# Heads, weight products and small loads of a branchformer backward kernel put in a hand-written order

## The chip, the cores and the metric

The kernel runs on one core of one Trainium2 chip. The metric is the device time of one execution in microseconds (us). The engines are called PE (TensorE, matrix products), PEld (its weight loads), DVE (VectorE), ACT (ScalarE), POOL (GpSimd) and SP (SyncE, which here only issues DMAs). Each engine works through its own queue of instructions in order and waits at an instruction until what it needs is there.

## What is computed

One layer and its gradients for x of shape (2, 4000, 144) in bf16. Two branches share a layer norm of x: an attention branch and a local branch with a gate and a convolution over 5 neighbours in time. Their results are merged by another convolution of 5 taps and a product. The kernel returns the output and the gradients of x and of all seven weights.

```python
xa = layernorm(x)
q, k, v = split(xa @ w_qkv)
glob = softmax(q k^T / sqrt(D)) v @ w_att_out
u, g = split(gelu(xa @ w_mlp_in))
loc = (u * conv5(layernorm(g), dw_csgu)) @ w_mlp_out
m = concat(glob, loc)
out = x + (m + conv5(m, dw_merge)) @ w_merge
# outputs: out, and d/d(x, w_qkv, w_att_out, w_mlp_in, dw_csgu, w_mlp_out, dw_merge, w_merge) for a given grad_out
```

## The kernel before

Time steps are tiled in 32 blocks of 128 rows; 4 blocks make a group, so there are 8 groups (NGR). The two batch entries are worked one after the other. Each has three phases: `phase_head`, `phase_attn` and `phase_tail`.

*Weights.* `Weights.first` loads the weights, transposes them on PE (`turn`, L1139, one PSUM tile and one DVE copy L1140 for each piece) and forms folded products (`fused`, L1148): M1 from the query and key weights, WvoT, and GL, which holds for each of the 5 taps the merge weights times a branch weight times the tap's factor. For GL, the branch weights are first scaled by each tap's factor: `A` for branch 0 on DVE (L1221), `A` for branch 1 and the small `Bz` on POOL (L1223, L1224), one instruction for each tap. `Weights.second` makes what is first needed later: transposes of Wo, Wi and Wm, the diagonals `w_dg` and `c80` of the convolution (`c80` from `w80`, ten DMAs of 16 elements), a flag (whether the fast path is allowed), WIM, copies of weights to DRAM, and G (ten products and ten ACT copies, L1337 and L1149, after ten small copies on POOL, L1332).

*Head.* For each group: `stA` takes `gs`, a load of grad_out rows with all 5 neighbours (720 KB, three slots, issued on SP by `take_go`), transposes its middle row (L1425), copies the 16 narrow columns together on POOL (`g80`, L1428) and transposes those (L1431, into go80, L1434). In batch 0 it also forms the norm of x: `stats` (DVE, L1367 and L1368), `power` (POOL, L1375 and L1376), `apply` (L1383 to L1388, on ACT, DVE and POOL); in batch 1 these were done in the tail before. `stT` transposes the normed x (L1439, L1443). `stB` handles two blocks: the query product pq (L1459, L1460) and pb (5 products L1467 and one L1468), copied out by DVE and ACT. Eight of the sixteen stB are done in the head; the rest are placed in the first rows of attention.

*Attention.* A written-out loop over 32 rows of blocks: scores (L1861, L1865), the exponential (ACT), a product (DVE), transposes by DMA (`flip`, SP), then y (L1911) and X (L1933, L1934). A list of small steps (`local_steps`) fills in the local branch. The first instruction of attention on PE is the pS product of L1861.

*Tail.* Steps h = 0 to 20 over pairs of blocks: turns (L2039, L2041, L2074), correlations EF (L2063), output products (L2088, L2089) and dx products (L2106). Narrow rows go to DRAM and come back shifted by `Taps`: `put` stores them (L1520) and `fill` loads them (L1527), both issued on ACT. `Taps` also writes two zero columns at each end, by two DMAs when it is made (L1514, L1515). The tail of batch 0 also prepares the norm of batch 1. The tail of batch 1 forms the weight gradients (`Finish`).

*Order.* Inside `tc.manual_schedule()` the instructions are queued as the code has them. Attention's loop and the tail's loop stand inside it. The weights, the heads, `local_steps`' opening instructions and the making of the `Taps` stand outside: there a planner chooses the order of each queue by its own priorities.

Of the kernel before, what the change touches and what calls it, by code (L numbers as in the profile page):

```python
# [1120 lines left out]
class Weights:  # L1121
# [6 lines left out]
    def turn(self, src, R, c0, C, name, ps, pool=None):  # L1128
        nc = self.k.nc
        nk, nck = (R + 127) // 128, (C + 127) // 128  # L1130
        t = (pool or self.tmp).tile([128, nck, R], BF, name=name)
        if C % 128:
            nc.vector.memset(t[:, nck - 1, :], 0.0)
        for cc in range(nck):
            w = min(128, C - cc * 128)
            for kt in range(nk):
                rk = min(128, R - kt * 128)
                pt = ps.tile([128, 128], BF, tag="tp", name="pt")
                nc.tensor.transpose(pt[0:w, 0:rk], src[0:rk, kt, c0 + cc * 128:c0 + cc * 128 + w], self.W.ident[0:rk, 0:rk])  # L1139
                nc.vector.tensor_copy(t[0:w, cc, kt * 128:kt * 128 + rk], pt[0:w, 0:rk])  # L1140
        return t
# [12 lines left out]
    def first(self, ps, then):  # L1154

        k, W, tp_, nc, wp = self.k, self.W, self.tmp, self.k.nc, self.k.wp
        c = float(D) ** -0.5
        W.ident = wp.tile([128, 128], BF, name="w_ident")
        make_identity(nc, W.ident[:])
        ident = W.ident  # L1160

        def load_k(ap, R, C, name, engs):
            nk = (R + 127) // 128
            t = tp_.tile([128, nk, C], BF, name=name)
            if R % 128:
                nc.vector.memset(t[:, nk - 1, :], 0.0)
            for kt in range(nk):
                r0, r1 = kt * 128, min(R, kt * 128 + 128)
                engs[kt].dma_start(t[0:r1 - r0, kt, :], ap[r0:r1, :])
            return t  # L1170
        W.Wqkv = load_k(k.w_qkv, D, 3 * D, "w_qkv_s", (nc.sync, nc.scalar))
        W.Wo = load_k(k.w_att_out, D, D, "w_o_s", (nc.sync, nc.scalar))
        self.Wl = load_k(k.w_mlp_out, D, D, "w_l_s", (nc.sync, nc.scalar))
        Wmh = self.Wmh = tp_.tile([128, 2, 2, D], BF, name="w_mh")
        nc.vector.memset(Wmh[:, :, 1, :], 0.0)
        for h in range(2):
            nc.sync.dma_start(Wmh[:, h, 0, :], k.w_merge[h * D:h * D + 128, :])
            nc.scalar.dma_start(Wmh[0:DR, h, 1, :], k.w_merge[h * D + 128:h * D + D, :])
        cw = tp_.tile([5, 3 * D], BF, name="w_cw")
        nc.scalar.dma_start(cw[:, 0:2 * D], k.dw_merge)  # L1180
        nc.scalar.dma_start(cw[:, 2 * D:3 * D], k.dw_csgu)
        then()
        self.Wi = load_k(k.w_mlp_in, D, 2 * D, "w_i_s", (nc.sync, nc.scalar))

        WqT = self.WqT = self.turn(W.Wqkv, D, 0, D, "w_qT", ps)
        WkT = self.WkT = self.turn(W.Wqkv, D, D, D, "w_kT", ps)
        WqTz = tp_.tile([128, 2, 128], BF, name="w_qTz")
        nc.vector.memset(WqTz[:], 0.0)
        nc.vector.tensor_copy(WqTz[:, :, 112:128], WqT[:, :, 128:D])
        W.M1 = wp.tile([128, 2, D], BF, name="w_M1")  # L1190
        self.fused(ps, lambda kt: WqT[:, kt, :], self.two(WkT), c, 0, 128, W.M1[:, 0, :])
        self.fused(ps, lambda kt: WqTz[:, kt, :], self.two(WkT), c, 0, 128, W.M1[:, 1, :])
        WvT = self.WvT = self.turn(W.Wqkv, D, 2 * D, D, "w_vT", ps)
        WlT = self.turn(self.Wl, D, 0, D, "w_lT", ps)
        self.WvoT = tp_.tile([128, 2, D], BF, name="w_voT")
        self.vo(ps, self.WvoT, W.Wo, WvT)

# [4 lines left out]
        for n_, dst in enumerate((W.wm[:, 0], W.wm[:, 1], self.wcf[:])):  # L1202
            pt = ps.tile([128, 128], BF, tag="tp", name="pt")
            nc.tensor.transpose(pt[:, 0:5], cw[0:5, n_ * D:n_ * D + 128], ident[0:5, 0:5])
            nc.tensor.transpose(pt[0:DR, 6:11], cw[0:5, n_ * D + 128:n_ * D + D], ident[0:5, 0:5])
            nc.vector.tensor_copy(dst[:, 0, :], pt[:, 0:5])
            nc.vector.tensor_copy(dst[0:DR, 1, :], pt[0:DR, 6:11])
        nc.vector.tensor_scalar(W.wm[:, :, :, 2], W.wm[:, :, :, 2], 1.0, None, op0=ALU.add)

        UT = self.UT = [self.WvoT, WlT]  # L1210
        W.GL = wp.tile([128, 5, 2, D], BF, name="w_GL")
        W.GL80 = wp.tile([128, 2, D], BF, name="w_GL80")
        self.A = []
        for h in range(2):
            A = tp_.tile([128, 2, 5, D], BF, name="w_A%d" % h)
            self.A.append(A)
            Bz = tp_.tile([128, 2, 5, DR], BF, name="w_Bz%d" % h)
            for kt in range(2):
                for kk in range(5):
                    if h == 0:  # L1220
                        nc.vector.tensor_scalar(A[:, kt, 4 - kk, :], UT[h][:, kt, :], W.wm[:, h, kt, kk:kk + 1], None, op0=ALU.mult)  # L1221
                    else:
                        nc.gpsimd.tensor_scalar(A[:, kt, 4 - kk, :], UT[h][:, kt, :], W.wm[:, h, kt, kk:kk + 1], 1.0, op0=ALU.mult, op1=ALU.mult)  # L1223
                    nc.gpsimd.tensor_scalar(Bz[:, kt, 4 - kk, :], Wmh[:, h, kt, 128:D], W.wm[:, h, kt, kk:kk + 1], 1.0, op0=ALU.mult, op1=ALU.mult)  # L1224
            for (m0, m1) in ((0, 3), (3, 5)):
                pt = ps.tile([128, 512], F32, tag="w", name="fw")
                n = (m1 - m0) * D
                for kt in range(2):
                    nc.tensor.matmul(pt[:, 0:n], Wmh[:, h, kt, 0:128], A[:, kt, m0:m1, :].rearrange("p a b -> p (a b)"), start=(kt == 0), stop=(kt == 1))
                (nc.scalar.copy if m0 else nc.vector.tensor_copy)(W.GL[:, m0:m1, h, :], pt[:, 0:n].rearrange("p (a b) -> p a b", b=D))  # L1230
            pt = ps.tile([128, 512], F32, tag="w", name="fw")
            for kt in range(2):
                nc.tensor.matmul(pt[0:80, 0:D], Bz[:, kt, :, :].rearrange("p a b -> p (a b)"), UT[h][:, kt, :], start=(kt == 0), stop=(kt == 1))
            nc.scalar.copy(W.GL80[0:80, h, :], pt[0:80, 0:D])
        W.mhalf = wp.tile([128, 4], F32, name="w_mhalf")
        nc.vector.memset(W.mhalf[:], -0.5)

    def vo(self, ps, t, l, r):
        self.k.nc.vector.memset(t[:, 1, :], 0.0)
# [4 lines left out]
    def second(self, pst, ps):  # L1244
# [4 lines left out]
        w80 = tp_.tile([128, 2], BF, name="w_w80")  # L1249
        nc.vector.memset(w80[:], 0.0)  # L1250
        with nc.allow_non_contiguous_dma(reason="small conv weights, channel on partitions"):
            for m in range(5):
                nc.sync.dma_start(w80[m * DR:(m + 1) * DR, 0:1], k.dw_csgu[m:m + 1, 128:D].rearrange("o c -> c o"))
                nc.sync.dma_start(w80[m * DR:(m + 1) * DR, 1:2], k.dw_csgu[4 - m:5 - m, 128:D].rearrange("o c -> c o"))
        w80f = tp_.tile([128, 2], F32, name="w_w80f")
        nc.vector.tensor_copy(w80f[:], w80[:])

        W.Wi2 = wp.tile([128, 2, 2 * D], BF, name="w_i2")
        nc.vector.memset(W.Wi2[:, 1, :], 0.0)
        nc.sync.dma_start(W.Wi2[:, 0, :], k.w_mlp_in[0:128, :])  # L1260
        nc.sync.dma_start(W.Wi2[112:128, 1, :], k.w_mlp_in[128:D, :])
# [8 lines left out]
        W.c80 = wp.tile([128, 2, DR], BF, name="w_c80")  # L1270
        for v in range(2):
            nc.vector.tensor_scalar(W.c80[:, v, :], i80[:], w80f[:, v:v + 1], None, op0=ALU.mult)

        WoT = self.turn(W.Wo, D, 0, D, "w_oT", pst)
        WiT = self.turn(self.Wi, D, 0, 2 * D, "w_iT", pst)
        WmT = tp_.tile([128, 2, 2, D], BF, name="w_mT")
        nc.vector.memset(WmT[:, :, 1, :], 0.0)
        for h in range(2):
            for cc in range(2):
                w = 128 if cc == 0 else DR  # L1280
                for kt in range(2):
                    rk = 128 if kt == 0 else DR
                    pt = pst.tile([128, 128], BF, tag="tp", name="pt")
                    nc.tensor.transpose(pt[0:w, 0:rk], Wmh[0:rk, h, kt, cc * 128:cc * 128 + w], ident[0:rk, 0:rk])
                    nc.vector.tensor_copy(WmT[0:w, h, cc, kt * 128:kt * 128 + rk], pt[0:w, 0:rk])
        Wvo = tp_.tile([128, 2, D], BF, name="w_vo")
        self.vo(ps, Wvo, self.WvT, W.Wo)

        M1k = tp_.tile([128, 2, D], BF, name="w_M1k")
        nc.vector.tensor_copy(M1k[:], W.M1[:])  # L1290
        fro = tp_.tile([128, 2], F32, name="w_fro")
# [104 lines left out]
def phase_head(k, W, b, S, nrm, ld, wts):  # L1396

    nc, tc = k.nc, k.tc
    with ExitStack() as es:
# [15 lines left out]
        def stA(g):  # L1415
            if g not in S.gs:
                take_go(k, S, b, g, ld)
# [1152 lines left out]
```

## Time and profile before

| what | value |
|---|---|
| median of 4 runs | 1295.7 us (1294.82 to 1297.4) |
| profiled execution | 1296.55 us, span 1294.7 us |
| PE / PEld busy | 1215.6 us (94%) / 952.3 us (74%) |
| DVE / ACT / POOL busy | 960.5 / 843.6 / 558.3 us |
| instructions | 39900 |
| bytes moved by DMA | 205.51 MB, 159 GB/s on average |

Lines of code are given as L and a number. A wait line reads "who waited <- who released it: us in total, number of times, longest". In a line of stretches, the numbers after the length are busy us of PE, PEld, DVE, ACT and POOL with the number of instructions, then the granted clock of PE as a share of full speed, the busy share of the DMA engines and GB/s. Idle time of an engine costs something only if the engine, or someone waiting for it, sets the end.

### The profile page before, as it was taken

How to read it: one execution, taken by the hardware profiler on the slowest of the kernel's cores; microseconds unless marked ns; L12 is line 12 of the kernel's file. 1: busy time of each engine (PE TensorE's matmuls, PEld its weight loads, DVE VectorE, ACT ScalarE, POOL GpSimd, SP SyncE). 2: the span in 40 equal slices, each digit the busy share in tenths (PEclk: the TensorE clock that was granted, in tenths of full speed). 3: DMA queues.
4: the chain of work that ended last, by engine and by line, in shares of the span. 5: the costliest groups of instructions: out<-in, count | busy, mean ns of one | idle time of the engine just before them, and what ended most of it. 6: DMA issues, size and time to landing. Idle time of an engine off the chain costs nothing.

```text
span 1294.7 us, 39900 instructions
## 1 busy us (share of the span) xinstructions
PE 1215.6 (94%) x15116; PEld 952.3 (74%) x15116; DVE 960.5 (74%) x3293; ACT 843.6 (65%) x2498; POOL 558.3 (43%) x1033
## 2 busy tenths in 40 slices
PE   4899999999999999989989999999999999998996
PEld 2657777777777777789976777777777777778884
DVE  4656778888888788857735677888878878885674
ACT  2667677767767766546646777777777777654542
POOL 6312444545444453256611244444544445324650
PEclk9989999999999999999989999999999999999998
DMA  6368989898989989887765898999899899997861
GB/s 184 87 133 147 155 157 160 158 165 149 164 145 163 169 155 162 150 186 217 203 213 108 147 157 150 151 170 166 147 165 153 158 165 156 162 154 181 239 163 30
DMA packets 634223, 205.51 MB, mean 159 GB/s; under 512 B 577183, under 2 KB 631556, under 8 KB 633988
## 3 DMA queue, kind: packets, MB, share of 16 engines
q1 hardware_dynamic: 627472, 197.54, 79.9%
q10 hardware_dynamic: 6548, 5.33, 1.7%
q8 instruction: 120, 1.97, 0.6%
q14 instruction: 83, 0.68, 0.2%
HBM read 46.22 MB, written 21.79 MB: 53 GB/s over the span
## 4 chain that ended last, share of the span: by engine, by line
PE 70%; DVE 13%; DMA 6%; ACT 4%; issue 4%; POOL 2%; SPq 1%; ACTq 0%; DVEq 0%; POOLq 0%
PE y L1911 15%; PE pS L1865 9%; PE X L1933 8%; PE X L1934 8%; PE pD L1865 7%; DVE Sm L1875 5%; PE pS L1861 5%; PE pc L1573 2%; PE pb L1467 2%; DVE jg L1792 1%; PE po L2088 1%; DMA y<-r 1%; PE gr L2159 1%; PE EF L2063 1%; DMA ug<-ug_d 1%
## 5 line engine op out<-in xcount | busy, mean ns | idle before, releaser
L1875 DVE SCALAR_TENSOR_TENSOR Sm<-pD,Pm 128x500 bf16<-128x500 f32 x512 | 325.8, 673 | 80.9 <-PE pD L1865 47.7
L1873 ACT ACTIVATE Pm<-pS 128x500 bf16<-128x500 f32 x512 | 295.4, 586 | 41.2 <-PE pS L1865 38.3
L1933 PE MATMUL X<-Qs,Sm 128*128 128x144 bf16 x2048 | 285.6, 226 | 9.3 <-DVE acc L1949 8.9
L1946 POOL TENSOR_TENSOR acc<-xs,acc 128x432 f32<-128x432 f32 x150 | 168.6, 1124 | 280.6 <-ACT xs L1945 280.2
L1934 PE MATMUL X<-Bt,Pm 128*128 128x144 bf16 x2048 | 285.4, 226 | 0.7 <-DVE Bt L1898 0.7
L1934 PEld LDWEIGHTS <-Pm 128*128 128x128 bf16 x2048 | 200.2, 98 | 11.9 <-issue 11.3
L1933 PEld LDWEIGHTS <-Sm 128*128 128x128 bf16 x2048 | 200.1, 98 | 1.5 <-issue 0.9
L1911 PEld LDWEIGHTS <-PT 128*128 128x128 bf16 x2048 | 136.5, 98 | 31.1 <-issue 2.4
L1911 PEld LDWEIGHTS <-ST 128*128 128x128 bf16 x2048 | 136.4, 98 | 27.6
L1945 ACT COPY xs<-X 128x432 f32<-128x432 f32 x150 | 77.9, 519 | 111.7 <-PE X L1934 103.6
L1949 DVE TENSOR_TENSOR acc<-X,acc 128x432 f32<-128x432 f32 x180 | 104.0, 578 | 54.1 <-PE X L1934 53.4
L1873 ACT ACTIVATION_READ_ACCUMULATOR Pm<-pS 128x1 f32 x512 | 104.9, 205 | 0.0
L1861 PE MATMUL pD<-rb,QBr 16*128 16x500 bf16 x448 | 96.0, 378 | 3.3 <-DVE Sm L1875 2.8
L1865 PEld LDWEIGHTS <-BTm 128*128 128x128 bf16 x512 | 49.8, 98 | 59.9 <-issue 1.6
L1861 PE MATMUL pS<-rb,QBr 16*128 16x500 bf16 x448 | 92.0, 381 | 0.1
L1792 DVE SCALAR_TENSOR_TENSOR jg<-gnC,dgC 128x256 bf16<-128x256 bf16 x160 | 89.0, 556 | 1.0
L1921 POOL TENSOR_TENSOR B_t<-zd,yd 128x144 bf16<-128x144 f32 x64 | 33.8, 528 | 113.2 <-ACT zd L1920 112.9
L1865 PEld LDWEIGHTS <-QTm 128*128 128x128 bf16 x512 | 29.0, 97 | 72.8 <-issue 72.8
L1865 PE MATMUL pS<-rb,QTm 128*128 128x500 bf16 x256 | 76.9, 382 | 0.0
L1865 PE MATMUL pS<-ra,QTm 128*128 128x500 bf16 x256 | 76.5, 380 | 0.0
L1911 PE MATMUL y<-rb,PT 128*128 128x144 bf16 x1024 | 74.3, 226 | 1.4 <-ACT zd L1920 1.1
L1911 PE MATMUL y<-ra,PT 128*128 128x144 bf16 x1024 | 74.3, 226 | 1.1 <-ACT zd L1920 1.1
(626 smaller groups left out, 2898.6 us busy)
## 6 DMA issues: line engine op xcount, KB each, us to landing
gs<-in_grad_out_dram SPq DMA_DIRECT2D x24, 720.0 KB
dh_d<-dh SPq DMA_DIRECT2D x32, 144.0 KB
dhr<-dh_d SPq DMA_DIRECT2D x16, 288.0 KB
gs<-in_grad_out_dram SPq DMA_DIRECT2D x8, 540.0 KB
xg<-in_x_dram SPq DMA_DIRECT2D x21, 144.0 KB
dug_d<-dug SPq DMA_DIRECT2D x16, 144.0 KB
dug<-dug_d SPq DMA_DIRECT2D x32, 72.0 KB
ug_d<-ug SPq DMA_DIRECT2D x32, 72.0 KB
```

The costliest lines, as they stand in the source:

```text
L1792: nc.vector.scalar_tensor_tensor(jg[:], a_[:, m:m + 256], 1.0, d_[:, 2:258], op0=ALU.mult, op1=ALU.mult, accum_out=dws[:, p, m:m + 1])
L1861: nc.tensor.matmul(o_[h][:, 0:SC], jt[i // 4][2][rr, i % 4, :], S.XR[c2][rr, 0:SC], start=True, stop=False)
L1865: nc.tensor.matmul(o_[h][:, 0:SC], jt[i // 4][w][:, i % 4, :], S.xaT[:, c0:c0 + SC], start=False, stop=True)
L1873: nc.scalar.activation(P[:, pb, c1:c1 + SC], o_[h][:, 0:SC], ACT.Exp, accum_out=ld8[:, 0, n_:n_ + 1])
L1875: nc.vector.scalar_tensor_tensor(Sm[:, pb, c1:c1 + SC], o_[h][:, 0:SC], 1.0, P[:, pb, c1:c1 + SC], op0=ALU.mult, op1=ALU.mult, accum_out=l ...
L1911: nc.tensor.matmul(y[:, w, :], src[:, jj, :], S.xaa[:, j, :], start=(j == 0), stop=(j == NBK - 1))
L1921: nc.gpsimd.tensor_tensor(S.Zn[:, i, :], zd[:], yd[:], op=ALU.add)
L1933: nc.tensor.matmul(X[:, jj, :], Sm[:, i % NP, j * 128:(j + 1) * 128], Qs[:, i % 4, :], start=(kk == 0 and jj == 0), stop=False, skip_group ...
L1934: nc.tensor.matmul(X[:, jj, :], P[:, i % NP, j * 128:(j + 1) * 128], Bt[:, i % 4, :], start=False, stop=(kk == 1), skip_group_check=True)
L1945: nc.scalar.copy(xs[:, 0:nj, :], X[:, 0:nj, :])
L1946: nc.gpsimd.tensor_tensor(a_, xs[:, 0:nj, :], a_, op=ALU.add)
L1949: nc.vector.tensor_tensor(a_, X[:, 0:nj, :], a_, op=ALU.add)
```

## The change

1. The weights and both heads are put inside `tc.manual_schedule()`. `first` and `second` become `loads`, `heads`, `taps`, `taps1`, `keys`, `rows` and `rest`; `rest` is a generator, of which one piece is queued in each step of the head's loop.
2. `turn` collects a transposed weight in one PSUM tile and copies it out in one or two instructions. The tap products for all five taps become one tensor-tensor instruction for each half (`taps` on DVE, `taps1` on POOL, `Bz` goes from POOL to DVE). G is copied out by four wide copies.
3. x of batch 0 comes in three loads (group 0, groups 1 to 3, groups 4 to 7) in place of eight, and w_merge in two in place of four. The loads are issued in the order weights for q, k, v, x of group 0, the other weights, then gs and x by turns; Wi is loaded once, later.
4. `c80` is formed by two small products with a pattern matrix; the ten DMAs of `w80` are gone.
5. The norm is split in `stats`, `power`, `shift` and `apply`, in different steps. `g80` is formed ahead by `narrow_go`. In batch 0 DVE's share of `apply` goes to POOL, and every second copy of R goes from DVE to ACT. The head's PSUM pools have 4 and 3 tiles instead of 3 and 4.
6. In the tail the `Taps` are made after the first loads, `fill` of a group moves from the odd step after it to the beginning of the next even step, the norm of batch 1 lags by one step more, `take_go` for batch 1 moves to the end of its step, and two `narrow_go` for batch 1 are put in its last steps.
7. `local_steps` is called inside the manual order.

```diff
 class Weights: turn
-                pt = ps.tile([128, 128], BF, tag="tp", name="pt")
-                nc.tensor.transpose(pt[0:w, 0:rk], src[...], self.W.ident[0:rk, 0:rk])
-                nc.vector.tensor_copy(t[0:w, cc, kt * 128:kt * 128 + rk], pt[0:w, 0:rk])
+                nc.tensor.transpose(pt[0:w, cc, kt * 128:kt * 128 + rk], src[...], self.W.ident[0:rk, 0:rk])
+        n1 = C // 128
+        nc.vector.tensor_copy(t[:, 0:n1, :], pt[:, 0:n1, :])
+        if C % 128:
+            nc.vector.tensor_copy(t[0:C % 128, n1, :], pt[0:C % 128, n1, :])
...
+    def taps(self):
+        for kt in range(2):
+            nc.vector.tensor_tensor(self.A[0][:, kt], self.UT[0][:, kt, :].unsqueeze(1).to_broadcast([128, 5, D]),
+                                    self.wr[:, 0, kt, :].unsqueeze(2).to_broadcast([128, 5, D]), op=ALU.mult)
+        for h in range(2):
+            for kt in range(2):
+                nc.vector.tensor_tensor(self.Bz[h][:, kt], ..., op=ALU.mult)
+    def taps1(self, kt):
+        self.k.nc.gpsimd.tensor_tensor(self.A[1][:, kt], self.UT[1]..., self.wr[:, 1, kt, :]..., op=ALU.mult)
...
+            nc.tensor.matmul(pt[0:80, v * DR:(v + 1) * DR], e5[0:5].rearrange("p a b -> p (a b)"), self.cw[0:5, 2 * D + 128:3 * D], start=True, stop=True)
+            nc.vector.tensor_tensor(W.c80[0:80, v, :], pt[0:80, v * DR:(v + 1) * DR], i80[0:80, :], op=ALU.mult)
...
 phase_head
+        with tc.manual_schedule():
...
+            if wts:
+                wts.heads(ps_t, ps_2, lambda: nrm.stats(0))
+                nrm.power(0)
+                wts.taps1(0)
+                wts.keys(ps_t, ps_2)
+                nrm.shift(0)
+                nrm.apply(0)
+                narrow(0)
+                wts.taps()
+                wts.taps1(1)
+                nrm.stats(1)
+                nrm.power(1)
+                stA(0)
+                take_go(k, S, b, 3, ld)
+                stT(0)
+                wts.rows(ps_2, 0)
+                nrm.shift(1)
+                nrm.apply(1)
+                narrow(1)
+                nrm.stats(2)
+                nrm.power(2)
+                wts.rows(ps_2, 1)
+                rest = wts.rest(ps_t, ps_2)
...
+            for n in range(-1, NGR):
+                if 1 <= n + 2 < NGR:
+                    stT(n + 2)
+                if n >= 0:
+                    stB(n, *tiles())
+                if 1 <= n + 2 < NGR:
+                    stA(n + 2)
+                if wts and n + 3 < NGR:
+                    nrm.shift(n + 3)
+                    nrm.apply(n + 3)
+                if n + 3 < NGR:
+                    narrow(n + 3)
+                if wts and n + 4 < NGR:
+                    nrm.stats(n + 4)
+                    nrm.power(n + 4)
+                if n + 5 < NGR and n + 5 not in S.gs:
+                    take_go(k, S, b, n + 5, ld)
...
+                if n == 5:
+                    spread()
+                if n == 3:
+                    jit()
+                if rest:
+                    next(rest, None)
 phase_tail
-        taps = [Taps(k, "y80_%d" % b), Taps(k, "u80_%d" % b)]
...
             loads(1)
+            taps += [Taps(k, "y80_%d" % b), Taps(k, "u80_%d" % b)]
...
                     turn_dx2(*turn_dx(h))
+                if hf == 0 and 0 <= g - 2 < NGR:
+                    fill(g - 2)
...
-                if hf == 1 and 0 <= g - 1 < NGR:
-                    fill(g - 1)
...
-                    for lag, f_ in ((4, nrm.apply), (3, nrm.power), (2, nrm.stats), (1, nrm.load)):
+                    for lag, f_ in ((5, nrm.apply), (4, nrm.shift), (3, nrm.power), (2, nrm.stats), (1, nrm.load)):
...
-                    if NPR <= h < NPR + 3:
-                        take_go(k, nxt, 1, h - NPR, nrm.ld)
+                    if NPR + 3 <= h:
+                        narrow_go(k, nxt, h - NPR - 3, nrm.ld)
...
+                if nrm and NPR <= h < NPR + 3:
+                    take_go(k, nxt, 1, h - NPR, nrm.ld)
 bounded (loads of batch 0)
+                        def put(n):
+                            if n == 0:
+                                nc.vector.memset(S.Sm[:, 1, 15 * D:16 * D], 0.0)
+                                wide(0, 1)
+                                return
+                            take_go(k, S, 0, 0, nrm.ld)
+                            wide(1, 4)
+                            take_go(k, S, 0, 1, nrm.ld)
+                            wide(4, NGR)
+                            take_go(k, S, 0, 2, nrm.ld)
```

## The prediction

> **What bounds the kernel now.** I read the page first: TensorE (PE) is busy 1215.6 of 1294.7 us, so only what leaves PE idle or slow can be won. The forty slices put the gap at the start. The stretches of 10 us there:
>
> ```profile
> 0.00:10.00 10.00, 0.60 (x4) 0.39 (x5) 3.56 (x36) 1.28 (x1) 2.51 (x15) 1.00 0.72 185
> 10.00:20.00 10.00, 8.20 (x56) 4.85 (x54) 6.57 (x42) 5.00 (x12) 7.47 (x20) 1.00 1.05 300
> 20.00:30.00 10.00, 2.97 (x18) 2.05 (x19) 2.04 (x10) 0.91 (x3) 9.49 (x37) 1.00 0.19 66
> 30.00:40.00 10.00, 8.04 (x77) 5.94 (x75) 6.93 (x37) 6.06 (x17) 4.68 (x10) 1.00 0.13 48
> 40.00:50.00 10.00, 7.09 (x81) 5.66 (x81) 7.45 (x44) 7.71 (x20) 6.28 (x12) 1.00 0.49 166
> 50.00:60.00 10.00, 9.35 (x96) 7.14 (x93) 5.60 (x23) 6.56 (x23) 2.04 (x4) 1.00 0.40 66
> 60.00:70.00 10.00, 9.96 (x60) 5.88 (x60) 2.97 (x20) 5.65 (x21) 0.62 (x2) 0.58 0.36 89
> ```
>
> The columns after the length are PE, weight load, DVE, ACT, POOL busy, then the granted clock, DMA share and GB/s. PE idles 9.4 + 1.8 + 7.0 + 2.0 + 2.9 + 0.7 = 23.8 us in the first 60 us; in 20 to 30 us POOL is full and everybody else is empty. The waits of that stretch (us in total, times, longest) and the chain of waits (start, length) say why:
>
> ```profile
> PE pr L1431 <- POOL g L1428: 8.6, 3, 7.0
> PE pm L1425 <- DMA gs<-in_grad_out_dram: 6.2, 1, 6.2
> SPq L1112 <- POOL w_A L1332: 8.9, 1, 8.9
> ```
>
> ```profile
> 18.54 2.41 POOL w_Bz L1224 x8
> ...
> 68.37 1.20 PE pb L1467 x5
> ...
> 73.34 0.61 PE pb L1467 x5
> ```
>
> PE takes its first transposes of batch 0's `gs` before most weight work, so it waits 6.2 us for that load; then POOL's twenty small tap products of L1223 and L1224 and ten copies of L1332 stand in front of the narrow copy L1428, which also keeps the gs slot and so the SP queue. Five products of L1467 take 1.20 us at 68 us and 0.61 at 73: PE runs at half speed around 66 to 73 us.
>
> The same head in batch 1 has no weights and no norms (they were made in the tail), and is my yardstick:
>
> ```profile
> 0.00:66.00 66.00, 42.21 (x366) 29.67 (x367) 35.04 (x208) 30.92 (x86) 32.77 (x95) 0.97 0.49 138
> 66.00:97.90 31.90, 30.58 (x210) 17.37 (x209) 17.48 (x63) 21.45 (x73) 5.00 (x8) 0.91 0.64 130
> 654.00:685.00 31.00, 25.96 (x276) 21.74 (x273) 12.22 (x36) 16.31 (x42) 5.63 (x16) 0.89 0.60 177
> 685.00:714.00 29.00, 27.65 (x206) 16.03 (x206) 17.22 (x60) 20.78 (x70) 4.69 (x7) 1.00 0.59 113
> ```
>
> In the tails ACT stands still for the r80 round trip, and PE for ACT (batch 1's tail); at the start of batch 1's head DVE waits for a store:
>
> ```profile
> ACT hT L2079 <- DMA u<-r: 4.5, 2, 3.3
> PE pt L2039 <- ACT hT L2079: 3.8, 4, 1.6
> DVE go80f L1434 <- DMA gr_d<-grs: 4.6, 1, 4.6
> ```
>
> **Head of batch 0, to the first attention score (L1861, now at 64.8 us).** I build the new time from rows.
>
> *Start.* `gs` of group 0 lands at 9.7 us now; it stays behind the same early loads, so PE's dense part starts at 9.9 (bounds 9 and 11). The weight work put ahead of it (16 + 6 transposes, 8 products of `heads` and `keys`, at 0.15 to 0.33 us some 6 us with their DVE copies) fits into the idle 2.8 to 9.7 us and costs nothing; were the chain through DVE longer, each us over comes on top, hence the 11.
>
> *Yardstick.* From PE's return at 659.85 to the first score at 684.97 is 25.1 us, plus 0.8 for the 12 transposes done before its wait: 25.9. It holds 5.8 us at half speed, which I leave in.
>
> *`rows`.* Twelve products, 3.3 us in the half-speed stretch 28.6 to 31.9: between 1.6 and 3.3, taken 2.4.
>
> *`rest`.* `second` holds PE from 58.4 to 66.4 us, 8.0 us with hand-offs and the clock's drop. Its 57 or so instructions at the 0.06 us spacing of full speed are 3.5. Spread over the loop, the hand-offs lie beside head work: taken 5, bounds 3.5 and 8. The ten DMAs of `w80` (0.42 us each on SP, 47 to 59 us) go; two small products replace them. G's ten evacuations of 0.29 us on ACT become four wide ones.
>
> *Norms.* Per group POOL has 0.19 + 1.02 (power) + 2 x 0.48 (apply) + 0.46 (narrow) = 2.6 us; ACT 0.58 + 0.57 + 0.40 + 0.56 + 1.0 + 0.3 (half of the R copies) = 3.4; DVE four times 0.29 + 0.17, 0.16, 0.41, 0.2, 0.6 = 3.2; against 2.8 us of PE per group in batch 1. ACT overruns PE by 0.6, though its starts overlap: taken 0.3 for each of 8 groups, 2.4 (bounds 0 and 4.8).
>
> *Taps.* On POOL, 20 x 0.295 + 10 x 0.384 = 9.5 us become two products of 128x720 with two inputs, which the trace does not show; the nearest row (L1722, two inputs, 128x576, 1.285) gives 1.6 each, its one-input neighbours 1.92 (5 x 0.384). DVE takes two of 128x720, 0.6 to 1.2 each by L1700's and L1726's 0.45 to 0.97 for 576, and four small ones. `rows(0)` waits for them, but stA(0) and stT(0) stand before it on PE.
>
> *First groups.* stT(1) needs x of group 1, then 1.8 (stats) + 1.2 (power) + 0.16 + 1.0 (apply) and some 0.5 of hand-offs. PE has about 5 us of work from 9.9. x now comes as 432 KB in one load behind gs. A 144 KB load took 2.35 us from issue to use, a gs load 5.4; so groups 1 to 3 arrive near 11.5, the chain ends at 16.2, and PE idles 1.3 or more: taken 3 (bounds 0 and 6).
>
> The Trainium skill, "DMA: Bandwidth & Descriptors" (Anatomy of one DMA), speaks against the wide load: the semaphore does not move until the last byte has landed, so group 1 waits for group 3's bytes. The trace has no such pair of loads; by the rule alone, an estimate, the start loses 1 to 2 us.
>
> Sum: 9.9 + 25.9 + 2.4 + 5 + 2.4 + 3 = 48.6, against 64.8: **-16.2** (ends 40.0 and 59.0, so -24.8 and -5.8).
>
> **First score to first y.** 64.8 to 97.9 is 33.1 us in batch 0, 685.0 to 714.0 is 29.0 in batch 1. The excess of 4.0 is the half-speed spell and the G products. With `rest` spread out I take 2.5 back (bounds 0 and 4): **-2.5**.
>
> "TensorE: Matmul & The Clock Gate" (What's actually happening) says the clock halves after an idle window of about 3.4 us. The spell at 66 us followed no PE gap above 0.7 us since 51.8, so the row differs from that rule; by the rule there was no cause to remove, and this term would be zero.
>
> **Tails.** `fill` moves from the odd step, where it waits on ACT for a store 5 us old, to the head of the next even one; hT, yT and the next store queue behind it on ACT. PE lost 3.8 + 0.7 to hT in one tail, 1.6 in the other: 6.1, of which I take 2.5 (bounds 0 and 6.1). The price: r80 has one step less before the out products. A step is 4.6 us, at the end (16 to 20) 2.9, and the stores of the same size took 3.4 to 5.4, so a late load can cost 2.5 in the last pair or two: taken 0.5, bound 5. The `Taps` columns leave SP's 67 to 79 us, where nobody waited, for 4 x 0.42 = 1.7 us behind loads(1); ahead of load_dh(2), and perhaps of the first `put`: 0 to 2 a tail, taken 0.25 each. `local_steps`' four and its load_R stand in place in front of the first flips, whose users come two rows later: nothing; uncovered 1.7 us. Net **-1.5**.
>
> **Head of batch 1.** go80f still overlays the gr_d store, so the 5 us stall stays; PE gets 20 transposes in instead of 12: **-0.5** (bounds -1 and +3, if the fixed order fits worse). The lag-5 apply and early narrow copies run on ACT and POOL under PE: nothing; uncovered 1.7 us, one group's apply.
>
> **Total.** 16.2 + 2.5 + 1.5 + 0.5 = 20.7. The profiled execution took 1296.55 us (span 1294.7 and 1.85 around it), 0.85 over the median of 1295.7; so 1275.0 in medians.
>
> **Rivals.** (1) *DMA sets the head.* By the last group 7.3 MB must have come. The stretch 10 to 20 us moved 300 GB/s, 0 to 66 us on average 138. At 138 the last group lands at 53, and about 5 us of PE work follow: head end 58, total 1287. For it: DMA share 1.05 there. Against it: the 138 comes with SP standing 8.9 us for a slot that POOL held.
> (2) *The fixed order serialises the norms: slower.* Place: PE's queue at stT(n+2). If each group's stats, power, shift, apply, transposes, copy and products ran one after the other, 1.8 + 1.2 + 0.2 + 1.0 + 0.4 + 0.6 + 1.5 and six hand-offs of 0.2 = 7.9 us for seven groups: 16.2 + 55 + 3.5 = 75, 10 us late; with 2 back from the tails 1304. It decides from about 5.7 us a group. Against it: the loop holds stats at n+4, shift at n+3, transposes at n+2, so an iteration carries a third of the chain. For it: four engines in strict order with nobody to fill gaps.
> (3) *Given back.* Weights and head are ready early, but attention's first rows wait on flips or spreads at SP, and little is left: a gain of 2, 1294. The 50 us stretches of attention show PE above 9 tenths, which speaks against it.
>
> **How the numbers follow.** Forecast 0.71, rival 1 0.15, rival 2 0.09, rival 3 0.05. Range 1266 to 1290: the low end is a gain of 30 (head 24.8 with the small terms), the high end takes in rival 1; what is left out is rivals 2 and 3 and a little below. 0.2% is 2.6 us, about what a measurement of this kernel can tell from no change: faster 0.88 (forecast, rival 1, part of 3), same 0.03, slower 0.09.
>
> **What would show it.** Right: PE idle in 0 to 60 us down from 24 to 10 or less, no stretch with POOL alone busy, the first score at 44 to 53 us and the first y near 79; POOL's w_A in two instructions near 1.6 us; no ACT wait on u<-r in the tails; the 4.6 us wait on gr_d still there. Wrong: groups spaced by over 5 us in the head's loop; PE waiting on gs loads after 20 us; out products waiting on r; a first score above 59.

## The result and the profile after

The changed kernel took 1296.8 us (median of 41 runs, 1292.6 to 1301.5), the kernel before 1294.2 us beside it (62 runs); the ratio is 1.0022 with a 95% interval of 1.0016 to 1.0029. The change is slower by 0.2%, where 20.7 us less were forecast. A second profile of each kernel was taken with the experiments (e15, e16), so that what belongs to the order can be told from what belongs to one execution. Stage by stage, in us of the span (the changes, means of two profiles, add up to 3.7; 0.0022 of 1295 is 2.8):

| stage (ends at) | before, two profiles | after, two profiles | measured change | forecast |
|---|---|---|---|---|
| head 0 (first score) | 64.7 / 63.7 | 61.5 / 60.6 | -3.2 | -16.2 |
| first score to first y | 33.0 / 32.3 | 29.0 / 28.8 | -3.8 | -2.5 |
| to the last y of batch 0 | 467.8 / 468.6 | 469.9 / 468.1 | +0.8 | 0 |
| tail 0 (to the copy of EF) | 72.0 / 71.5 | 78.7 / 78.4 | +6.8 | -0.75 |
| head 1 (first score) | 47.5 / 46.7 | 43.7 / 44.8 | -2.9 | -0.5 |
| to the last y of batch 1 | 497.4 / 498.5 | 498.0 / 498.2 | +0.2 | 0 |
| tail 1 (to EF of batch 1) | 69.3 / 68.1 | 71.8 / 74.6 | +4.5 | -0.75 |
| the end | 43.1 / 43.0 | 44.2 / 44.3 | +1.2 | 0 |

The stretches of the start in the changed kernel, columns as before:

```profile
0.00:10.00 10.00, 4.77 (x30) 2.61 (x30) 6.69 (x51) 2.14 (x5) 5.85 (x17) 1.00 0.68 138
10.00:20.00 10.00, 6.11 (x40) 3.99 (x41) 6.16 (x27) 4.24 (x12) 6.31 (x9) 1.00 1.06 281
20.00:30.00 10.00, 8.98 (x64) 5.92 (x61) 5.80 (x28) 5.25 (x14) 4.70 (x9) 0.66 0.61 202
30.00:40.00 10.00, 8.48 (x94) 6.57 (x93) 7.03 (x36) 8.37 (x26) 7.12 (x16) 1.00 0.58 183
40.00:50.00 10.00, 4.50 (x44) 3.68 (x43) 4.51 (x24) 4.52 (x11) 6.04 (x19) 0.78 0.32 108
50.00:60.00 10.00, 9.38 (x95) 7.50 (x93) 3.67 (x11) 5.82 (x17) 1.95 (x5) 0.87 0.27 35
```

The stretch with POOL alone is gone, and PE idles 17.8 us instead of 23.8. But 3.9 us of that idleness lie at 10 to 20 and 5.5 at 40 to 50 us, and the clock column now shows 0.66 at 20 to 30 and 0.78 and 0.87 at 40 to 60 us. (Before, it stood at 1.00 up to 60 us; but the trace's record of the clock begins only at 30.9 us there and at 18.4 us in the changed kernel, so the 1.00 ahead of these is no measurement.) PE's waits in 0 to 62 us name the places:

```profile
PE tp L1472 <- DMA gs<-in_grad_out_dram: 3.1, 1, 3.1
PE fw L1359 <- POOL w_e L1358: 3.0, 1, 3.0
PE pm L1485 <- ACT ra L1428: 2.4, 5, 0.6
PE pj L1537 <- DVE QB L1533: 2.1, 1, 2.1
```

The first is SP's queue. In the kernel before, the four pieces of group 0's gs were issued without a break, from 3.74 to 5.27 us. The timeline in the changed kernel (start, length of the issue):

```profile
3.46 0.38 SPq L1107 DMA_DIRECT2D gs<-in_grad_out_dram  x1
4.20 0.35 SPq L1620 DMA_DIRECT2D gnC_d<-w_zero  x1
4.59 0.42 SPq L1621 DMA_DIRECT2D gnC_d<-w_zero  x1
...
5.99 0.43 SPq L1107 DMA_DIRECT2D gs<-in_grad_out_dram  x1
6.99 0.30 SPq L1620 DMA_DIRECT2D gnC_d<-w_zero  x1
7.39 0.40 SPq L1108 DMA_DIRECT2D gs<-in_grad_out_dram  x1
8.10 0.52 SPq L1110 DMA_DIRECT2D gs<-in_grad_out_dram  x2
8.67 0.40 SPq L2619 DMA_DIRECT2D Sm<-in_x_dram  x1
```

gs of group 0 comes in four pieces (L1107, L1108, two of L1110). Between the first and the rest stand five zero columns of `local_steps`' Taps and the first gs load of tail 0 (5.99 us, 540 KB). The written order holds within one written region; these five columns and this load belong to later regions and wait for nothing, and the planner queued them in between. Probably it expected SP to wait there for the memset of the gs tile on POOL: with the tile cleared elsewhere the pieces stay together (e5_start below). In the trace that memset ends at 3.26 us, so nothing was gained by it.

The second and fourth wait are seen in the chain of waits of the changed kernel (start, length):

```profile
41.65 0.23 DVE st L1403
...
43.70 1.01 POOL rstdx L1412
44.71 0.54 POOL w_A L1344 x2
46.82 0.27 POOL w_e L1358
47.14 0.24 PE fw L1359
...
49.31 1.20 PE pb L1513 x5
...
55.19 0.61 PE pb L1513 x5
```

On DVE the copies into QB stand behind the statistics of group 7, and on POOL the pattern `e5` (w_e) stands behind the norm's power, two wide tap copies and the selects of i80. PE does 0.4 us of work between 41.6 and 47.1 us. Its products take double time until 52.5 us (1.20 for five, 0.61 after).

In the tails the chain shows what the prediction had at 0.25 us (tail 0; in tail 1 the columns took 3.44 us in place of 5.00):

```profile
564.66 0.42 SPq L1620
565.12 5.00 DMA y<-w_zero
570.22 0.34 ACTq L1626
570.68 0.39 ACTq L1626
571.11 1.02 ACT hT L2185
572.18 1.14 PE po L2212 x8
```

The first `put` (L1626, on ACT) stores into the same DRAM tile that the zero columns go to, and waits until they have landed; hT is queued behind it on ACT, and PE waits for hT. In tail 0 of the kernel before and then of the changed one:

```profile
PE po L2106 <- ACT hT L2079: 0.8, 2, 0.4
```

```profile
PE po L2212 <- ACT hT L2185: 5.0, 2, 4.6
ACT hT L2185 <- DMA u<-w_zero: 5.4, 1, 5.4
```

### The profile page after: what moved, and what is told of

It is laid out like the page before. It is cut to its first block, busy times and chain, and to the rows that moved or that the text cites. A ratio compares the mean times of both kernels' runs of the same rounds, so it can differ in the third digit from the quotient of the medians.

```text
span 1296.8 us, 39808 instructions
## 1 busy us (share of the span) xinstructions
PE 1219.3 (94%) x15118; PEld 958.1 (74%) x15118; DVE 961.7 (74%) x3258; ACT 844.4 (65%) x2494; POOL 558.0 (43%) x1009
## 4 chain that ended last, share of the span: by engine, by line
PE 70%; DVE 14%; ACT 5%; DMA 4%; issue 4%; SPq 1%; POOL 1%; ACTq 0%; DVEq 0%; POOLq 0%
PE y L2017 15%; PE pS L1971 9%; PE X L2039 8%; PE X L2040 8%; PE pD L1971 7%; PE pS L1967 5%; DVE Sm L1981 5%; PE pb L1513 3%; PE pc L1679 2%; PE po L2194 2%; PE EF L2169 2%; DVE jg L1898 1%; PE gr L2265 1%; DVE acc L2055 1%; PE pD L1967 1%
## 5 line engine op out<-in xcount | busy, mean ns | idle before, releaser
L1971 PEld LDWEIGHTS <-BTm 128*128 128x128 bf16 x512 | 49.8, 98 | 59.9 <-issue 1.6
```

The lines of the kernel that those rows point to most:

```text
L1971: nc.tensor.matmul(o_[h][:, 0:SC], jt[i // 4][w][:, i % 4, :], S.xaT[:, c0:c0 + SC], start=False, stop=True)
```

## The experiments

Ratios are to the kernel before on the same chip, with 95% intervals. Theory A is that single waits of the order took the gain (zero columns in the tails, constants and loads in the head); its rivals are the moved `fill` (B) and the pace of the norms (C). "Units" count the half-speed spells that began before the first y: each unit is 3.4 us at a clock of 0.50, at most 1.7 us lost. The two profiles of the kernel before have 3 and 2, those of the changed one 4 and 4. Slow work ahead of the first entry of the clock record (15.0 us in e14 to 36.5 us in e3) is not in the count. First score, first y, units and tails are from one profiled execution of each kernel, medians and ratios from all its runs.

| kernel | median | ratio | first score / y | units | tail 0 / 1 |
|---|---|---|---|---|---|
| e1_taps_back | 1286.8 | 0.9926 (0.9910 to 0.9942) | 60.6 / 89.5 | 4 | 73.2 / 67.9 |
| e2_before_taps | 1313.1 | 1.0133 (1.0114 to 1.0153) | 64.3 / 98.8 | 3 | 77.0 / 74.7 |
| e3_before_fill | 1296.7 | 1.0007 (0.9993 to 1.0021) | 66.9 / 101.4 | 2 | 73.5 / 66.8 |
| e4_consts | 1295.5 | 0.9993 (0.9979 to 1.0007) | 57.4 / 87.0 | 3 | 78.3 / 73.2 |
| e5_start | 1295.6 | 1.0003 (0.9988 to 1.0017) | 56.5 / 86.0 | 3 | 78.8 / 73.3 |
| e6_pace | 1296.0 | 1.0002 (0.9985 to 1.0020) | 60.7 / 89.7 | 5 | 79.2 / 74.9 |
| e7_norms_out | 1290.8 | 0.9962 (0.9945 to 0.9978) | 52.6 / 81.6 | 1 | 78.9 / 71.9 |
| e8_all | 1283.1 | 0.9901 (0.9878 to 0.9923) | 51.9 / 81.1 | 0 | 71.9 / 69.8 |
| e9_fill_back | 1287.6 | 0.9936 (0.9923 to 0.9949) | 55.3 / 84.0 | 2 | 78.9 / 70.9 |
| e10_split | 1284.6 | 0.9912 (0.9893 to 0.9931) | 57.7 / 87.1 | 4 | 72.0 / 67.8 |
| e11_rest_end | 1286.7 | 0.9926 (0.9913 to 0.9939) | 52.7 / 87.0 | 3 | 74.0 / 67.1 |
| e12_apply_back | 1281.5 | 0.9891 (0.9877 to 0.9905) | 55.1 / 84.7 | 2 | 73.2 / 66.5 |
| e13_tail_back | 1292.6 | 0.9982 (0.9968 to 0.9997) | 58.2 / 88.1 | 4 | 77.8 / 68.5 |
| e14_best | 1282.0 | 0.9892 (0.9870 to 0.9913) | 54.8 / 85.4 | 4 | 72.4 / 66.6 |
| e17_lag4 | 1287.3 | 0.9946 (0.9930 to 0.9962) | 59.9 / 88.7 | 3 | 71.2 / 69.6 |

**The tails.** e1 undoes one line of the changed kernel, e2 does it alone on the kernel before:

```diff
 e1 (e2: the reverse, on the kernel before)
-        taps = []
+        taps = [Taps(k, "y80_%d" % b), Taps(k, "u80_%d" % b)]
...
             loads(1)
-            taps += [Taps(k, "y80_%d" % b), Taps(k, "u80_%d" % b)]
```

> The changed kernel with one thing undone: the two Taps of each tail are made where the kernel before made them, outside the written order. Theory A (the tails lost to the zero columns): in the changed kernel the first `put` stands on ACT's queue until the zero columns have landed (the chain has 5.00 us of DMA y<-w_zero), hT behind it, and PE waits 4.6 and 4.5 us for hT once in each tail. Without that, 4.6 + 4.5 = 9.1 us come back, and with the clock's spells at 571 to 578 and 1192.6 to 1196 us (half speed for 6.8 and 3.4 us, so 3.4 and 1.7 lost) up to 14: 1296.8 - 9 to 14 = 1283 to 1288. Rival B (the moved `fill` is what costs, the zero columns only show where it waits): 1294 to 1298.

> The kernel before with one part of the change alone: the two Taps of each tail are made in the written order, behind loads(1). Theory A: the first `put` waits for the zero columns here too, since it stands at the same place on ACT's queue: about 5 us in each tail and perhaps a spell of the clock, 1294.2 + 9 to 14 = 1303 to 1308. Rival B (only together with the moved `fill`): 1293 to 1297.

Both as theory A has it: 12.4 us back ((1.0022 - 0.9926) x 1295), and 17 us lost, more than the 9 to 14 expected (the profiled execution lost 9.3; the runs spread over 9 us; where the rest of the 17 went is not shown). PE's wait in e1's tail 0 (555 to 634 us):

```profile
PE po L2212 <- ACT hT L2185: 0.8, 2, 0.4
```

The moved `fill`, alone on the kernel before (e3), and undone on kernels with the tails' Taps early (e9 on e8_all, e13 on e1_taps_back):

```diff
 e9, e13 (e3: the reverse, on the kernel before)
-                if hf == 0 and 0 <= g - 2 < NGR:
-                    fill(g - 2)
...
                     put(g)
+                if hf == 1 and 0 <= g - 1 < NGR:
+                    fill(g - 1)
```

> The kernel before with another part alone: `fill` at the head of the even step after next. The prediction's term: 2.5 us won of the 6.1 us that PE waits for hT and yT, 0.5 lost to a late r80, so about 1292.2. Theory A': the move is worth that or more, 1291 to 1293. Rival B: it costs, because the out products then wait on r80 or because fill's issue now stands in front of hT, 1296 or more.

> The kernel of e8_all with `fill` back at the odd step, so everything of the tails as before the change. If the prediction's term for the moved `fill` (2.5 won, 0.5 lost) holds, this is 2 us slower than e8_all: 1285. If the move is worth nothing (e3: 1.0007 of before alone): 1283, within 1.

> The changed kernel with Taps and `fill` of the tails as before, so the changed head alone. Against e1_taps_back (1286.8, 0.9926 of before) it prices the moved `fill` once more. If the move is worth what e9_fill_back lost (4.5 us): 1291, 0.996. If it is worth nothing, as e3_before_fill said: 1287, 0.9926.

Alone it gave nothing (e3's tails add up to 140.3 us, those of the kernel before to 141.2 and 139.6; its first score and first y are late in a head whose order is that of the kernel before, so that is the execution and not the edit). Undone it cost 4.5 us (e9 against e8), which neither of e9's expectations had, and 7 us (e13 against e1), most of it in tail 0 (7.0 and 4.6 us in the profiles). ACT's timeline in e13 shows why:

```profile
591.91 0.40 ACTq L1633 DMA_DIRECT2D r<-y  x1
592.40 0.39 ACTq L1633 DMA_DIRECT2D r<-u  x1
592.84 1.70 ACT L1428 ACTIVATE rb<-xg,nm,rstdx 128x144 bf16<-128x144 bf16 x4 [0.58 <-POOL ve L1411]
594.45 0.99 ACT L2185 COPY hT<-pt 128x1024 bf16<-128x1024 bf16 x1
```

The change's lag of 5 puts the four applies of batch 1's norm into the odd steps, where `fill` stood; with `fill` still there both stand ahead of hT, and PE waits:

```profile
PE pt L2145 <- ACT hT L2185: 5.4, 5, 1.9
```

e17, on the kernel of e13, moves the apply back too:

```diff
-                    for lag, f_ in ((5, nrm.apply), (4, nrm.shift), (3, nrm.power), (2, nrm.stats), (1, nrm.load)):
+                    for lag, f_ in ((4, nrm.shift), (4, nrm.apply), (3, nrm.power), (2, nrm.stats), (1, nrm.load)):
```

> The kernel of e13_tail_back with shift and apply of batch 1's norm back at a lag of 4 steps (even steps), so `fill` and apply are apart again, as in the kernel before. If the two moves of the change belong together (each alone puts fill's wait and 1.70 us of apply in the same step on ACT): tail 0 goes from 77.8 back to 72 to 73 us, the time is 1287 to 1288 (0.993). If the moved `fill` earns its gain by itself: it stays at e13_tail_back's 0.998, 1292.

Tail 0 went from 77.8 to 71.2 us, and the ratio to 0.9946, near the 0.993 expected. In tail 0 neither move wins by itself: the moved `fill` alone took 73.5 us (e3) against 72.0 and 71.5, the lag of 5 alone 77.8 (e13) against 71.2 (e17), and both together 73.2 (e1).

**The head.** e4 takes i80 and e5 from `rest` into `loads`, e5_start clears the first gs tile early, e6 and e7 add to e4:

```diff
 e4_consts: rest
-        i80 = tp_.tile([128, DR], BF, name="w_i80")
-        nc.gpsimd.memset(i80[:], 0.0)
...
+        i80 = self.i80
...
+            e5 = self.e5[v]
 e5_start
+        S.gs[0] = nrm.ld.tile([128, 4, 5, D], BF, tag="gs", name="gs")
+        nc.vector.memset(S.gs[0][:, 0, :, :], 0.0)
         wide(0, 1)
 e6_pace, on e4_consts
+                if wts and n + 3 < NGR:
+                    nrm.shift(n + 3)
+                    nrm.apply(n + 3)
                 if 1 <= n + 2 < NGR:
                     stT(n + 2)
...
+                if n == 3:
+                    wideQB()
                 if wts and n + 4 < NGR:
                     nrm.stats(n + 4)
 e7_norms_out, on e4_consts with wideQB: stats (power and shift alike)
+        if not self.b and g:
+            self.t[g].append(None)
+            return
```

> The changed kernel, the head's constants i80 and e5 (memsets and affine selects on POOL) issued at the start, where POOL idles 3 us, and not in the fifth part of `rest`. Theory A (head): PE's wait of 3.0 us for e5 and the 0.3 behind it go, and with the idle stretch 44.1 to 47.1 us goes the half-speed spell of 45.7 to 52.5 us (3.4 lost); the 2.1 us wait for QB stays: 1296.8 - 5 to 7 = 1290 to 1292. Rival C (the norms' chain of 4.2 us a group through ACT sets the head, and what one wait gives, the next group takes): a gain of 2 or less, 1295 or more.

> The changed kernel, only the memset of the first gs tile moved: on DVE at the very start (it stood on POOL behind the identity). In the changed kernel five zero-column DMAs and the 540 KB of a tail's first gs load stand on SP between the pieces of group 0's gs (4.20 to 7.4 us), and in front of x of groups 1 to 3; with the tile cleared early they queue behind. Theory D: gs of group 0 lands at 9.7 us as before, not 12.9, x of groups 1 to 3 near 11.5, not 15.0; the first score comes 3 us earlier (58.5), and the time is 1293 to 1294.5. Rival C (the groups' pace takes it back): less than 1 us, 1296.

> The kernel of e4_consts with two more moves in the head's order: the copies into QB on DVE ahead of the statistics of group 7 instead of behind, and each group's shift and apply ahead of the products of the group three earlier, not behind (one step more for ACT). Theory A: PE's waits for QB (2.1 us) and for xaa (pm<-ra, 2.5 us in five) go; the first score comes at 57.4 - 4.6 = 53 us, the time is 1290 to 1292. Rival C (four engines in a fixed order: the copies B_t and go80 that now stand behind the apply become late): waits move to pb, pq or tp, and the first score stays above 56, 1294 or more.

> The kernel of e4_consts with QB moved as in e6_pace, the apply where the changed kernel has it, and with work left out: the norm statistics, power and shift of groups 1 to 7 of batch 0 (constants stand in their place; the apply stays). It prices the term that the prediction put at 2.4 us (bounds 0 and 4.8). By the prediction: first score 57.4 - 2.1 - 2.4 = 53. Rival (2) of the prediction, the fixed order serialises the norms: 45 to 49. If the statistics cost PE nothing beyond QB's wait: 55.

e4 won 3.7 us against the changed kernel (1.0022 to 0.9993), between A's 5 to 7 and C's 2. The 3.3 us on the pattern `e5` went, QB's 2.1 and 2.5 of pm <- ra stayed. e5_start put the queue right (the last piece of gs is issued at 4.78 us, not 8.10; PE's first transposes of it start at 10.33 us, not 12.91) and won 2.5 us in the median, the lower end of what was expected. But PE's dense part began at 13.23 us, as late as ever: behind the first transposes it now waits 2.3 us for POOL's narrow copy, which stands behind apply. What came earlier is group 1's statistics, 12.4 us instead of 15.0. e6 won nothing over e4: the waits on QB and ra became 1.9 us on B_t, 1.6 on go80f and 1.4 on go80l, as C has it. e7, without the statistics of groups 1 to 7, is 4.0 us faster than e4, QB's wait included; the prediction's term for the norms (2.4) plus QB (2.1) makes 4.5. The first score came at 52.6 us, as the prediction's terms had it (53); rival (2), for which it would have come at 45 to 49, is out: the fixed order does not serialise the norms at 7.9 us a group. A part of the 4.0 us may be the clock: e4's profile has three units, e7's one.

> All moves together on the changed kernel: the tails' Taps made early (e1), the constants early (e4), QB and the apply earlier (e6), the first gs tile cleared on DVE (e5). If the parts add up: 1286.8 - 3.7 - 4.6 - 3 = 1275 to 1277, the first score near 50, the first y near 79. If the groups' pace gives some back: 1279 to 1283.

The parts as measured nearly add up: 12.4 + 3.7 + 2.5 - 1.2 = 17.4, and e8 is 15.7 us under the changed kernel. The expected 1275 to 1277 was missed, since QB and the earlier apply (e6) gave nothing of the 4.6 us counted on; 1283.1 is the end of the other case. Four more kernels vary e8:

```diff
 e10_split
-                            wide(1, 4)
+                            for g_ in (1, 2, 3):
+                                wide(g_, g_ + 1)
 e11_rest_end: `rest` runs behind the loop
-                if rest:
-                    next(rest, None)
 e12_apply_back: shift and apply behind stA again, as the change has them
 e14_best, on e12: the five dg products behind c80, and
-            if self.b or j % 2 == 0:
+            if self.b or j % 2 == 0 or g == 0:
```

> The kernel of e8_all with x of groups 1 to 3 in three loads of 144 KB where the change has one of 432 KB. By the rule weighed in the prediction (the semaphore moves only with the last byte) group 1's statistics start 1 to 2 us earlier and the time falls by as much, to 1281.5. If POOL's narrow copy and not x holds PE at 10.5 to 13.2 us (as e8_all's waits say: PE tp <- POOL g 2.3): no change, within 1, and two more issues on SP (0.9 us) in front of the next gs.

> The kernel of e8_all with `rest` in one piece behind the loop, as `second` stood before the change, its POOL constants still early. It prices the spreading: the prediction took 5 us for `rest` in the loop and 8.0 in a row. Then the first score comes 3 us later (55), the time is 1286. If PE waits for the norms' chain in the loop anyway and `rest` only fills those waits: 6 to 8 us later, 1289 to 1291.

> The kernel of e8_all with each group's shift and apply where the change has them. e6_pace showed no gain from moving them (1.0002 of before, against 0.9993 without QB's and this move) and PE waits of 1.9 us on B_t and 1.4 on go80f in their place. If the move is worth nothing: 1283, within 1.5. If PE's waits pm <- ra (2.4 us) come back and nothing goes: 1285.

> The kernel of e12_apply_back with two moves: the five dg products on DVE behind c80 instead of ahead (PE fw <- w_c waits 2.0 us there), and all four applies of group 0 on ACT (POOL's two take 2.43 us beside DVE's wide tap product, and its narrow copy, for which PE waits 2.3 us, stands behind them). If both waits are on the path: 1281.5 - 3 to 4 = 1277.5 to 1278.5. If the norms' chain takes it back: 1281 or more.

e10: no gain; nobody on PE's path waits for group 1's x. e11: 3 to 4.5 us slower, not in the first score (52.7, where 55 was expected) but in the place it had before: 34.2 us from there to the first y (29.2 in e8), up to 3.2 of them by a spell of two units at 52.3 us. e12: the moved apply was worth nothing; at 0.9891 it has the lowest ratio of the study, 1.1% under the kernel before, though e14 and e8 lie within its interval. e14: the waits of 2.3 and 2.0 us fell to 0.3 and 1.2, pm <- ra rose from 1.6 to 2.2, two units of half speed more came (at 18.4 and 83.2 us), and the time stayed.

**The clock.** 

> The changed kernel itself, a second profile. If the two half-speed spells of the head (21.8 to 28.6, 45.7 to 52.5 us) belong to its order, they are there again, since PE's 3.0 us wait ahead of the second is; the first score is within 1 us of 61.5. If they belong to the execution, their number differs, and the first score moves by 1.7 us for each 3.4 us of half speed more or less.

> The kernel before, a second profile. Its first y stood at 97.9 us with one spell of 10.2 us at half speed (61.6 to 71.8, 5.1 lost). If the spell belongs to the order: again there, first y within 1 us. If it belongs to the execution: another number of spells, and the first y earlier or later by 1.7 us for each.

The changed kernel has both spells again, 6.8 us each, at 20.8 and 44.7 us, and the first score at 60.6. PE works through the same head in e1, e13 and e17, and there too spells begin at 20.8 to 23.3 and at 41.5 to 44.7 us: that there are two belongs to the order. Their length does not: the five profiles have 4, 4, 4, 3 and 3 units before the first score, which comes at 58.2 to 61.5 us. In the kernel before, the spell is there again at 62 us with two units instead of three, and the first y is 1.7 us earlier. Nor is a stall needed: e8 and e10 differ in one load, both without the wait on the pattern `e5`, and their stretches of 20 to 30 and 40 to 50 us read (e8 first, then e10):

```profile
20.00:30.00 10.00, 8.21 (x88) 6.47 (x88) 7.46 (x39) 6.57 (x18) 6.01 (x12) 1.00 0.51 147
40.00:50.00 10.00, 8.74 (x106) 7.58 (x106) 5.41 (x20) 8.53 (x24) 3.78 (x9) 1.00 0.55 127
```

```profile
20.00:30.00 10.00, 9.53 (x82) 7.01 (x82) 5.89 (x33) 4.81 (x14) 4.55 (x9) 0.83 0.50 150
40.00:50.00 10.00, 7.13 (x55) 5.34 (x53) 5.25 (x28) 7.04 (x18) 6.17 (x13) 0.66 0.36 111
```

With 0, 2 and 4 units in e8, e12 and e10 the first y stands at 81.1, 84.7 and 87.1 us. The trace shows in e10 two units (42.9 to 49.7 us) where the changed kernel has its second spell, so that the wait sets that spell off is not shown.

## Why the prediction was wrong

**Tails, -1.5 forecast, +11.3 measured: the step that cost most.** It priced the Taps' columns by their issue on SP (4 x 0.42 us, taken 0.25 a tail) and asked who is behind them on SP. It named the first `put`, but as standing behind those issues; it did not ask who waits for the columns to land: that same `put`, on ACT, ahead of hT. It had named hT as queued behind ACT's DMAs, but for `fill` only. The landing took 5.0 us in tail 0 and 3.4 in tail 1, PE's waits 9.1 us, and some 12 us of the time went there (e1, e2). The other term, for `fill` (-2.0 with its price), is not there either: with the Taps early, both tails together take 139.0 to 141.7 us (e1, e8, e10, e12, e14), before 139.6 and 141.2. What the moved `fill` does is make room for the apply: with `fill` in its old step the lag of 5 costs 6.6 us in tail 0 (e13 against e17), with `fill` moved next to nothing (e1 against e3), so the "nothing" for that lag holds only together with the move.

**Head of batch 0, 48.6 forecast, 61.5 measured.** Five terms of its sum make up most of the difference of 12.9:
- Start, 9.9 taken, 12.9 measured (+3.0, above the bound of 11). "It stays behind the same early loads" was wrong: loads of other regions still came in between. e5_start mends the loads.
- `rows`, 2.4 taken, 3.4 measured (+1.0), all at half speed.
- `rest`, 5 taken: its POOL constants, which nothing in the sum priced, cost 3.3 (+3.3).
- Norms, 2.4 taken: 2.4 of pm <- ra and 2.1 for QB behind the statistics (+2.1, inside the bound of 4.8).
- The clock: the yardstick's 5.8 us at half speed (2.9 lost) were left in; the head has two spells of 6.8 us, in which PE was busy for 11.0 us (5.5 lost, +2.6).

These are 12.0; the rest of the sum holds to within 1. With the loads, the constants and QB mended, the head is 51.9 us in e8, without a spell, and 55.1 in e12, with two units: inside the bounds of 40 and 59, so the yardstick was usable. But the 9.6 us from 61.5 to e8's 51.9 are not all stalls that the written order made: 5.5 are the half speed, of which e8 has none, and about 4 are left for the stalls. In the time the three stalls come to 3.7 (e4), 2.5 (e5_start) and nothing (e6). Of the shortfall of 23.5 us (20.7 and 2.8), e1 gives back 12.4 and e12 another 4.5; what is left is about e12's head against 48.6.

Two readings of the prediction were off without weight in its sum: 20 x 0.295 + 10 x 0.384 is 9.7, not 9.5, and the spell put at 66 us runs from 61.6 to 71.9 in the trace's clock record.

**First score to first y, -2.5 forecast, -3.8 measured: right in sign and inside its bounds.** How the excess divides between the G products and the half speed, the two causes that the prediction named, stays open: e11 puts the G products behind the loop and has 34.2 us again, but with the spell noted above; e3 has 34.6 with one unit in that stretch. The Trainium skill, "TensorE: Matmul & The Clock Gate" (What's actually happening), by which this term would be zero, does not decide it: the changed kernel has no spell in this stretch and two in the head.

**The Trainium skill, "DMA: Bandwidth & Descriptors" (Anatomy of one DMA)**, by which the wide load loses 1 to 2 us, is not seen in e10 (0.9912 against 0.9901 and 0.9891): x of group 1 was not what PE waited for. That section describes DMAs that GpSimd issues, and these loads are issued on SP; e10 tests what the load cost the kernel, not the rule.

**Head of batch 1, -0.5 forecast, -2.9 measured**, with the stall on gr_d still there (4.2 us against 4.6); not taken apart. POOL's w_A came in two instructions of 1.39 us (1.6 forecast). Not expected: the 1.2 us after the last EF. The last computing instruction, on DVE, ends 36.7 us behind EF in both kernels, so they lie in the closing waits behind it; why is open.

**The rivals.** "Given back" (1294) came nearest in time, but what it named, attention's first rows waiting at SP, is not there: 29.0 us from the first score to the first y is batch 1's time. The groups' spacing was over 5 us three times (6.0, 10.1 and 5.9 us from one pb to the next), as rival (2) would have it, but with the two spells and the stall on QB and `e5` in them; e7 speaks against the norms in series. The range ended at 1290, with 0.09 for slower, because each unknown was bounded alone, while the wrong steps were unnamed waits that all go one way.

## What to carry to other kernels

When a DMA is moved later, price its landing for everyone who waits for the data or stores into the same tile, and look at what is queued behind the waiter, not only at the issue. An order written by hand must place one-time constants and small copies (here on POOL and DVE) ahead of recurring work, or their user waits behind it (3.0 and 2.1 us here). Read one profile of a head like this with care: with the same order its first score came anywhere between 58.2 and 61.5 us. Undo each line of a large change alone: one line of this one cost 12 us, and without it the change is 0.7% faster than before, and 1.1% with the head mended.

## What the runs showed of the hardware

- Half-speed spells last 3.41, 6.83 or 10.24 us: one, two or three units of 3.4 us at a granted clock of 0.50. The Trainium skill, "TensorE: Matmul & The Clock Gate" (What's actually happening), has an activity window of about 3.4 us and two clock states, which agrees. Its condition for the slow state, an idle window, does not always agree: the changed kernel's spells began with PE busy for 0.79 (21.8 us), 0.12 (45.7), 0.00 (571.3) and 0.39 (585.0) of the 3.2 us before, and the spells at 61.6 us of the kernel before and at 710.6 us of its second profile with 0.99 and 0.87. Ahead of the spell at 21.8 us all 26 matrix instructions on PE were transposes (25 of 25 ahead of e12's at 21.8 us); whether these count as work for the clock no run here tests, and at 710.6 us none was a transpose.
- The clock column is not the whole story: at 13.4 to 14.7 us the changed kernel's sets of four transposes took 0.43 us each with a clock of 1.00, and 0.22 at 32.0 us. The record of the clock begins at 18.4 us there.
- 80 rows of two elements (0.3 KB) took 3.4 to 6.0 us from the end of their issue to the user, in the six tails of the changed kernel's two profiles and e2.
- POOL's two applies took 2.43 us at 9.5 us, while DVE ran two products of 128x720 (1.71), and 0.92 elsewhere. The Trainium skill, "GPSIMD Engine Reference" (Specifications), says that POOL shares its SBUF interfaces with DVE and contends with DVE's instructions of two SBUF inputs, which agrees.
